# Attention and a gated FFN on one core: q and k laid out transposed by numpy, low parts on GpSimd, P divided on VectorE, V's product a step later

## The chip, the cores and the metric

The kernel runs on one core of one Trainium2 chip. The metric is device time in microseconds, the median of three runs. The engines are called as the profile calls them: PE (TensorE; PEld is its weight load), DVE (VectorE), ACT (ScalarE), POOL (GpSimd) and SP (SyncE, whose queue issues nearly all DMAs).

## What is computed

Eight-head attention over 4 sequences of 768 tokens with head size 64, with a window of 96 keys and 8 global keys and a linear bias by distance, and behind it an FFN whose gate is a ratio of polynomials:

```
scores = q @ k.T / 8 - slope[h] * dist          # where keep, else -1e9
a = exp(scores - max); a = a / (sum(a) + 1e-9)
x = (a @ v) as [3072, 512]
h = x @ w_in                                    # [512, 2048], float64 input
g = (a0 + a1*h + a2*h**2 + a3*h**3) / (1 + |b0|*|h| + |b1|*h**2 + 1e-6)
out = g @ w_out                                 # [2048, 512], float64 input
```

## The kernel before

The work is cut in two streams that are woven together. A **unit** u is one pair of heads (p, two heads x = 0, 1) for 128 query rows (block i of a sequence); 96 units, 8 to a chunk of 256 tokens. An **FFN tile** f is 256 of the 2048 hidden columns for one chunk; also 96. A loop over steps t issues each unit's stages and, with a lag that `turn(f)` gives (10 steps at first, growing to LAG = 13 between tiles 16 and 24), each tile's stages. A scheduler then sets each engine's order from the priorities (1000 for a step plus the numbers in PRI), so the built order is not the order of the code.

The first 24 units (PLAIN) run in plain float32. From unit 24 on, q and k are split in a high part that PE takes in its reduced-precision float32 format (fp32r) and a low part, so that a score is two matmuls (line 439). For these units the stages are:

- `st_load` (L137): q and k of two units come as they lie in memory, `nat`; `st_move` (L146) copies them within SBUF through a DMA into `mv`, whose type PE may transpose.
- `st_qkT` (L377): four PE transposes for two units, `tk` in PSUM (L384), through the identity `ident_r`.
- `st_qkE` (L396): for each unit and each of its heads ACT writes the high part into `kq` (L416, 64 partitions, q and k side by side) and DVE the low part into the other 64 partitions (L417), both with the factor 2^(p-1). Two DMAs then build `qT` with the halves exchanged (L421, L422).
- `st_score` (L427): four score matmuls (L439), then DVE adds the mask (bf16, scaled by the head's slope) and takes the row maximum (L453). Before this, POOL puts the 8 global keys in (L444).
- `st_soft` and `st_sums`: exponentials on ACT (L463), sum and reciprocal on DVE (L468, L470).
- `st_norm` (L472): POOL divides P, two instructions of 128x256 for a unit (L479).
- `st_turn` (L495): DVE turns P in 32x32 blocks (L504), a DMA writes it to DRAM (`put`), and `st_back` (L511) reads it back with the blocks exchanged (`pT`).
- `st_pv` (L525): V's product for four units at once (L541), issued at step u + 8; `st_x` splits x into `xh` and `xl` (L570, L571).

The FFN tile f goes through `st_ffn1` (24 matmuls, L272), `st_ew1` (three ACT instructions from `h`), `st_ew2` (L303, L304 on DVE; the sum `fa` on POOL, L305), `st_ew3` (1/Q as exp(-log) on ACT, L312, L313), `st_ew4` (L317 to L319 on DVE, `g` high on ACT, L327, `g` low on POOL, L328) and `st_ffn2` (12 matmuls, L348). The weights are decoded and split (`split_w`, L223, L224) in the first 180 us.

Of the kernel before, what the change touches and what calls it, by code (L numbers as in the profile page):

```python
# [19 lines left out]
G = 8  # L20
# [6 lines left out]
LAG = 13  # L27
# [51 lines left out]
def window_masks(nc, scr, mask0, masks, nl, ng):  # L79
# [24 lines left out]
    nc.vector.tensor_copy(out=masks[:, 2, :], in_=masks[:, 0, :])  # L104
# [3 lines left out]
def tile_kernel(ctx: ExitStack, tc: tile.TileContext, q, k, v, n_global, n_local,  # L108
# [28 lines left out]
    def st_load(u, other=nc.sync):  # L137
        c, t, p, b, i = unit(u)
        hs = slice(2 * p, 2 * p + 4)
        r = slice(i * P, (i + 1) * P)  # L140
        n = pl.ldp.tile([P, 2, 4, D], F32, tag="nat", name=f"nat{u}")
        nc.sync.dma_start(out=n[:, 0], in_=q[b, hs, r, :].rearrange("h s d -> s h d"))
        other.dma_start(out=n[:, 1], in_=k[b, hs, r, :].rearrange("h s d -> s h d"))
        nat[u // 2] = n

    def st_move(u):  # L146
        n = pl.late.tile([P, 2, 4, D], FR, tag="moved", name=f"mv{u}")
        nc.sync.dma_start(out=n.bitcast(F32), in_=nat[u // 2])
        nat[u // 2] = n
# [246 lines left out]
    def st_qkE(u):  # L396
# [30 lines left out]
    def st_score(u):  # L427
# [3 lines left out]
        for x in range(2):  # L431
# [5 lines left out]
            rhs = pl.kq[:, h, 0:2, :] if i else pl.kq[:, h, 0:1, :].broadcast_to([P, 2, P])  # L437
            for z, lhsT in enumerate((pl.kq[:, h, 2, :], qT[:, x, :])):
# [3 lines left out]
        elif 1 <= i < NT - 1:  # L442
            hs = slice(2 * p, 2 * p + 2)
            nc.gpsimd.tensor_copy(out=pl.kq[:, hs, i % 2, 0:G], in_=pl.kG[:, hs, :])  # L444

        def mask(x):
            m0, m = (mask0, masks) if u < PLAIN or x == 0 else (pl.half0, pl.halves)
            return m0 if i == 0 else m[:, 0:2, :] if i % 2 else m[:, 1:3, :]
        pr = pl.att.tile([P, 2, 2, P], F32, tag="prob", name=f"pr{u}")
        st = stats[:, u % 4]  # L450
        for x in range(2):
# [125 lines left out]
    def windowed(lates):  # L577
# [18 lines left out]
        nc.vector.tensor_copy(out=ident_r, in_=ident)  # L596
        one = pl.early.tile([1, P], F32, name="one")
# [9 lines left out]
        window_masks(nc, scr, mask0, masks, nl, ng)  # L607
# [4 lines left out]
        def halve_masks():  # L612
            for m, full_m in ((pl.halves, masks), (pl.half0, mask0)):
                nc.vector.tensor_scalar(out=m, in0=full_m, scalar1=0.5, scalar2=None, op0=ALU.mult)

        def turn(f):
            return f + EARLY_LAG + (LAG - EARLY_LAG) * min(max(f - 2 * FPC, 0), FPC) / FPC

        f = -1
        for t in range(NU + LAG + F2 + 1):  # L620
# [22 lines left out]
            if t % 2 == 0:  # L643
                on("load", st_load, t + 4)
# [8 lines left out]
            if t == PLAIN:  # L653
                scope.close()
                pl.late = lates.enter_context(tc.tile_pool(name="late", bufs=1))
                pl.kq = pl.late.tile([P, H, 3, P], FR, name="kq")
                pl.kG = pl.late.tile([P, H, G], FR, name="kG")
                pl.halves = pl.late.tile([P, 3, P], BF16, name="halves")
                pl.half0 = pl.late.tile([P, P], BF16, name="half0")
# [207 lines left out]
```

## Time and profile before

| | us |
|---|---|
| median of 3 runs | 732.49 (732.41 to 733.73) |
| the profiled execution | 732.77 |
| its span, first to last instruction | 730.9 |
| PE busy | 706.0 (97%) |
| DVE busy | 604.1 (83%) |
| ACT busy | 577.1 (79%) |
| POOL busy | 457.5 (63%) |

A row of a view of groups gives line, engine, operation, the tiles it writes and reads, shape, count, then busy time in us and the mean of one in ns, then the engine's idle time before it and what ended it. Matmuls overlap in their records, so how long PE takes for one is read from start to start in the timeline. The sum of busy times says which engine is near its limit; the windows say in which stretch.

### The profile page before, as it was taken

To read this page: it belongs to the slowest core of one execution; us is meant where nothing else is said; L and a number is where in the kernel's file an instruction comes from. 1 tells how busy PE (TensorE), PEld (TensorE's weight loads), DVE (VectorE), ACT (ScalarE), POOL (GpSimd) and SP (SyncE) were. 2 spreads that over 40 slices of the span, in tenths; PEclk is the share of its full clock that TensorE was granted. 3 is DMA by queue.
4 is the path that set the end of the run, shared out by engine and by line. 5 is a ranking of instruction groups with operands and counts; after the bars stand their busy time and mean duration, and the time that the engine had idled before them with its cause. 6 is when DMAs were issued, how large, how long until landed. Compare 5 with 4: busy or idle time off the path is not lost.

```text
span 730.9 us, 14868 instructions
## 1 busy us (share of the span) xinstructions
PE 706.0 (97%) x4762; PEld 608.0 (83%) x4762; DVE 604.1 (83%) x1508; ACT 577.1 (79%) x1304; POOL 457.5 (63%) x504
## 2 busy tenths in 40 slices
PE   5898999999999999999999999999999999999996
PEld 4575666788978889988988998998998998988894
DVE  5789966789889898888889889898889988875664
ACT  6798576977988788888887878887888878865764
POOL 3275986767567675665566657665667666754441
PEclk9999999999999999999999999999999999999998
DMA  9987210114564654645536455665346454421001
GB/s 265 294 278 215 89 23 22 52 23 105 157 166 133 200 154 130 182 141 154 142 111 181 140 136 166 173 183 137 98 121 197 138 160 129 118 88 30 30 1 34
DMA packets 139899, 96.76 MB, mean 132 GB/s; under 512 B 84260, under 2 KB 124196, under 8 KB 139812
## 3 DMA queue, kind: packets, MB, share of 16 engines
q1 hardware_dynamic: 138608, 95.20, 45.4%
q8 instruction: 40, 0.66, 0.4%
q10 hardware_dynamic: 1204, 0.52, 0.3%
q14 instruction: 47, 0.39, 0.2%
HBM read 53.22 MB, written 23.59 MB: 105 GB/s over the span
## 4 chain that ended last, share of the span: by engine, by line
PE 83%; DVE 6%; ACT 5%; DMA 2%; issue 2%; POOL 0%; SPq 0%; DVEq 0%; ACTq 0%; POOLq 0%
PE h L272 32%; PE acc L348 32%; PE o L541 5%; PE s L439 4%; PE acc L343 2%; PE h L264 2%; PE s L434 2%; DMA r<-in_moe_w_in_dram 1%; ACT pr L463 1%; PE tk L384 1%; PE tp L492 1%; DVE fu L303 1%; DVE fu L319 1%; DVE pr L453 1%; DMA nat<-in_q_dram 1%
## 5 line engine op out<-in xcount | busy, mean ns | idle before, releaser
L272 PE MATMUL h<-xh,win_l 128*128 128x256 f32 x704 | 197.1, 280 | 0.0
L479 POOL TENSOR_SCALAR pr<-pr,stats 128x256 f32<-128x256 f32 (+1 forms) x176 | 156.2, 898 | 59.5 <-DVE stats L470 37.0
L305 POOL TENSOR_TENSOR fa<-fa,fs 128x512 f32<-128x512 f32 x95 | 123.7, 1302 | 92.0 <-ACT fs L298 86.5
L348 PE MATMUL acc<-wout_l,g 128*128 128x512 f32 x352 | 139.3, 396 | 0.0
L328 POOL TENSOR_TENSOR g<-fu,g 128x512 fp32r<-128x512 f32 x87 | 113.9, 1309 | 33.9 <-ACT g L327 31.1
L272 PEld LDWEIGHTS h<-xh,win_l 128*128 128x128 f32 x704 | 133.2, 189 | 1.8 <-issue 0.5
L463 ACT ACTIVATE pr<-pr,stats 128x256 f32<-128x256 f32 (+1 forms) x192 | 93.1, 488 | 18.5 <-DVE stats L453 17.2
L296 ACT ACTIVATE fu<-h,coef 128x512 f32<-128x512 f32 (+1 forms) x97 | 74.9, 772 | 39.5 <-PE h L272 34.5
L317 DVE SCALAR_TENSOR_TENSOR fu<-fu,coef,q 128x512 f32<-128x512 f32 (+1 forms) x97 | 71.4, 736 | 32.5 <-ACT q L313 30.6
L312 ACT ACTIVATE fs<-fa,coef 128x512 f32<-128x512 f32 (+1 forms) x97 | 69.6, 717 | 22.5 <-POOL fa L305 21.1
L303 DVE TENSOR_TENSOR fu<-fu,h 128x512 f32<-128x512 f32 (+1 forms) x97 | 65.0, 671 | 21.0 <-ACT fs L298 20.7
L348 PEld LDWEIGHTS acc<-wout_l,g 128*128 128x128 f32 x352 | 66.2, 188 | 11.8
L304 DVE SCALAR_TENSOR_TENSOR fu<-fu,coef,h 128x512 f32<-128x512 f32 (+1 forms) x97 | 71.4, 736 | 1.9
L318 DVE SCALAR_TENSOR_TENSOR q<-fa,coef,q 128x512 f32<-128x512 f32 (+1 forms) x97 | 72.1, 743 | 0.0
L417 DVE SCALAR_TENSOR_TENSOR kq<-tk,kq 64x256 fp32r<-64x256 f32 x144 | 60.6, 422 | 10.9 <-ACT kq L416 6.7
L416 ACT ACTIVATE kq<-tk 64x256 fp32r<-64x256 f32 x144 | 54.2, 376 | 19.2 <-DVE kq L417 13.6
L297 ACT ACTIVATE fa<-h,coef 128x512 f32<-128x512 f32 (+1 forms) x97 | 65.6, 676 | 1.4 <-DMA out_dram<-o 1.3
L298 ACT ACTIVATE fs<-h,coef 128x512 f32<-128x512 f32 (+1 forms) x97 | 66.2, 682 | 0.3 <-DVE q L318 0.2
L319 DVE SCALAR_TENSOR_TENSOR fu<-q,fu 128x512 f32<-128x512 f32 (+1 forms) x97 | 65.2, 672 | 1.3
L327 ACT CAST g<-fu 128x512 fp32r<-128x512 f32 (+1 forms) x89 | 54.9, 616 | 13.3 <-DVE fu L319 12.2
L504 DVE STREAM_TRANSPOSE tb<-pr 128x256 f32<-128x256 f32 (+1 forms) x144 | 58.7, 414 | 5.7 <-POOL pr L479 2.0
L313 ACT ACTIVATE q<-fs 128x512 f32<-128x512 f32 (+1 forms) x97 | 57.3, 591 | 2.0 <-DVE stats L470 0.6
(257 smaller groups left out, 1943.8 us busy)
## 6 DMA issues: line engine op xcount, KB each, us to landing
put<-tb SPq DMA_DIRECT2D x30, 512.0 KB
pT<-put SPq DMA_DIRECT2D x120, 128.0 KB
mv<-nat SPq DMA_DIRECT2D x36, 256.0 KB
qT<-kq SPq DMA_DIRECT2D x144, 64.0 KB
r<-in_moe_w_in_dram SPq DMA_DIRECT2D x16, 512.0 KB
r<-in_moe_w_out_dram SPq DMA_DIRECT2D x16, 512.0 KB
nat<-in_q_dram SPq DMA_DIRECT2D x48, 128.0 KB
vt<-in_v_dram SPq DMA_DIRECT2D x48, 128.0 KB
```

The lines of the kernel that those rows point to most:

```text
L272: nc.tensor.matmul(out=hps[f][:, y, :], lhsT=w[:, fs], rhs=x[:, ct, :], start=(n == 0), stop=(n == 3 * NCT - 1))
L296: nc.scalar.activation(out=u, in_=h, func=AF.Identity, scale=a3, bias=a2)
L303: nc.vector.tensor_tensor(out=u, in0=u, in1=h, op=ALU.mult)
L304: nc.vector.scalar_tensor_tensor(out=u, in0=u, scalar=a1, in1=h, op0=ALU.add, op1=ALU.mult)
L305: side(f).tensor_tensor(out=a, in0=a, in1=s, op=ALU.add)
L317: nc.vector.scalar_tensor_tensor(out=u, in0=u, scalar=a0, in1=r, op0=ALU.add, op1=ALU.mult)
L318: nc.vector.scalar_tensor_tensor(out=r, in0=a, scalar=q1, in1=r, op0=ALU.add, op1=ALU.mult)
L319: nc.vector.scalar_tensor_tensor(out=u, in0=r, scalar=2.0, in1=u, op0=ALU.subtract, op1=ALU.mult, reverse0=True)
L328: side(f).tensor_tensor(out=g[:, 1, ys], in0=u, in1=g[:, 0, ys], op=ALU.subtract)
L348: nc.tensor.matmul(out=acc, lhsT=gs[f][:, z, y, ts], rhs=w, start=(ft == 0 and n == 0), stop=(ft == NFT - 1 and n == 2))
L463: nc.scalar.activation(out=d, in_=d, func=AF.Exp, scale=-1.0, bias=st[:, x:x + 1], accum_out=st[:, 2 + 2 * x:3 + 2 * x])
L479: nc.gpsimd.tensor_scalar(out=d, in0=d, scalar1=st[:, 6 + x:7 + x], scalar2=None, op0=ALU.mult)
```

## The change

From unit 24 on:

- numpy builds one more input, `qk`, in which q and k of four heads stand already transposed, [128 of two heads' dimensions, (k, q), two units, 128 rows]. One DMA of 2 KB a partition loads it for two units, two steps ahead instead of four. `st_move`, the four transposes and `tk` are gone.
- `st_split` takes the place of `st_qkE` and works on two units at once: two ACT casts of 64x512 from SBUF, and two subtractions of 64x512, now on POOL. The factor 2^(p-1) is dropped; in its place each head has its own copy of the mask, scaled on DVE once at step 24 (seven instructions). `qT` is built by two DMAs for two units, their priority 600 later, in place of four.
- The division of P (`st_norm`) is DVE's.
- `st_turn` turns a unit's two heads in one instruction of 512 columns.
- V's product is issued at t % 4 == 1, at step u + 9. LAG is 14, and `turn` lets the lag grow from tile 8 to tile 24 instead of from 16 to 24.

Before unit 24, and in the FFN, nothing is changed but the lag and where the mask lies.

```diff
-LAG = 13
+LAG = 14
...
+        if u >= PLAIN:
+            nat[u // 2] = pl.ldp.tile([P, 2, 2, P], F32, tag="nat", name=f"kq{u}")
+            nc.sync.dma_start(out=nat[u // 2], in_=qk[b, i, p // 2])
+            return
...
-    def st_move(u):
-        n = pl.late.tile([P, 2, 4, D], FR, tag="moved", name=f"mv{u}")
-        nc.sync.dma_start(out=n.bitcast(F32), in_=nat[u // 2])
-        nat[u // 2] = n
...
-        if u >= PLAIN:
-            tk = pl.ps_t.tile([P, 2, 2, P], FR, tag="t", name=f"tk{u}")
-            for y in range(2):
-                for z in range(2):
-                    n = nat[u // 2][:, 1 - z, 2 * y:2 * y + 2, :]
-                    nc.tensor.transpose(out=tk[:, y, z, :], in_=n.rearrange("p a d -> p (a d)"), identity=ident_r)
-                tqk[u + y] = tk[:, y]
-            return
...
+    def st_split(u):
+        c, t, p, b, i = unit(u)
+        kq, raw = pl.kq, nat[u // 2]
         for x in range(2):
             own, other = slice(x * D, (x + 1) * D), slice((1 - x) * D, (2 - x) * D)
-            at = kq[:, 2 * p + x, i % 2:3:2 - i % 2, :]
-            nc.scalar.activation(out=at[own], in_=raw[own], func=AF.Copy, scale=half)
-            nc.vector.scalar_tensor_tensor(out=at[other], in0=raw[own], scalar=half, in1=at[own], op0=ALU.mult,
-                                           op1=ALU.subtract)
-        hs = slice(2 * p, 2 * p + 2)
-        qT = pl.late.tile([P, 2, P], FR, tag="qT", name=f"qT{u}", bufs=4)
-        nc.sync.dma_start(out=qT[0:D].bitcast(F32), in_=kq[D:P, hs, 2, :].bitcast(F32))
-        nc.sync.dma_start(out=qT[D:P].bitcast(F32), in_=kq[0:D, hs, 2, :].bitcast(F32))
+            at = kq[:, x, p // 2, i % 2:3:2 - i % 2]
+            nc.scalar.copy(out=at[own], in_=raw[own])
+            nc.gpsimd.tensor_tensor(out=at[other], in0=raw[own], in1=at[own], op=ALU.subtract)
+        tc.cur_priority += 600
+        qT = pl.late.tile([P, 2, 2, P], FR, tag="qT", name=f"qT{u}", bufs=2)
+        nc.sync.dma_start(out=qT[0:D].bitcast(F32), in_=kq[D:P, :, p // 2, 2].bitcast(F32))
+        nc.sync.dma_start(out=qT[D:P].bitcast(F32), in_=kq[0:D, :, p // 2, 2].bitcast(F32))
...
-            rhs = pl.kq[:, h, 0:2, :] if i else pl.kq[:, h, 0:1, :].broadcast_to([P, 2, P])
-            for z, lhsT in enumerate((pl.kq[:, h, 2, :], qT[:, x, :])):
+            kx = pl.kq[:, x, p // 2, :, p % 2, :]
+            rhs = kx[:, 0:2, :] if i else kx[:, 0:1, :].broadcast_to([P, 2, P])
+            for z, lhsT in enumerate((kx[:, 2, :], qT[:, x, :])):
...
-            nc.gpsimd.tensor_scalar(
+            (nc.vector if u >= PLAIN else nc.gpsimd).tensor_scalar(
                 out=d, in0=d, scalar1=st[:, 6 + x:7 + x], scalar2=None, op0=ALU.mult)
...
-            for x in range(2):
-                at = 2 * y + x
-                nc.vector.transpose(out=turned[:, :, at:at + 4 * W - 3:4, :].rearrange("p b w i -> p w b i"),
-                                    in_=pr[:, x, 0:W, :].rearrange("p w (b j) -> p w b j", j=Q))
+            at = turned[:, :, 2 * W * y:2 * W * (y + 1), :].rearrange("p b n i -> p n b i")
+            if i:
+                nc.vector.transpose(out=at, in_=pr.rearrange("p x w (b j) -> p (x w) b j", j=Q))
...
+        def scaled_mask(h):
+            if 0 <= h < H and h != 2:
+                nc.vector.tensor_scalar(out=masks[:, h], in0=masks[:, 2], scalar1=2.0 ** (2 - h), scalar2=None,
+                                        op0=ALU.mult)
...
-            return f + EARLY_LAG + (LAG - EARLY_LAG) * min(max(f - 2 * FPC, 0), FPC) / FPC
+            return f + EARLY_LAG + (LAG - EARLY_LAG) * min(max(f - FPC, 0), 2 * FPC) / (2 * FPC)
...
-                on("load", st_load, t + 4)
+                if t + 4 < PLAIN:
+                    on("load", st_load, t + 4)
+                if t + 2 >= PLAIN:
+                    on("load", st_load, t + 2)
...
-            if t % 4 == 0 and t - 8 >= PLAIN:
-                pv(t - 8, 0)
+            if t % 4 == 1 and t - 9 >= PLAIN:
+                pv(t - 9, 0)
...
-                on("qkE", st_qkE, t)
-                on("qkE", st_qkE, t + 1)
+                on("qkE", st_split, t)
```

In the rows of the built order below a name's number tells one buffer from another; `s` are scores, `h` and `acc` the FFN's sums, `fa` and `g` the FFN's sum on POOL and its result.

PE, in the middle of the attention stretch, around the scores of a pair, before:

```order
L348 MATMUL acc_0_5353<-wout_l,g_5266 128x512
L439 MATMUL s_5372<-kq,qT_5230 128x256
L439 MATMUL s_5372<-kq 128x256
L439 MATMUL s_5372<-kq,qT_5230 128x256
L384 MATMUL tk_5398<-ident_r,mv_5217 128x128 x4
L348 MATMUL acc_0_5353<-w_0h,g_5266 128x512
```

and after:

```order
L430 MATMUL s_5239<-kq 128x256
L430 MATMUL s_5239<-kq,qT_5006 128x256
L430 MATMUL s_5239<-kq 128x256
L430 MATMUL s_5239<-kq,qT_5006 128x256
L430 MATMUL s_5318<-kq 128x256
L430 MATMUL s_5318<-kq,qT_5192 128x256
L430 MATMUL s_5318<-kq 128x256
L270 MATMUL h_5068<-xh_4409,w_0_1h 128x256
```

The four transposes of a pair are gone, and scores of several units follow one another.

DVE, there, for about one unit, before:

```order
L453 ISA pr_5499,stats<-s_5493,halves 128x256
L453 ISA stats 128x1
L317 SCALAR_TENSOR_TENSOR fu_5466<-fu_5466,coef,q_5524 128x512
L318 SCALAR_TENSOR_TENSOR q_5524<-fa_5467,coef,q_5524 128x512
L468 TENSOR_REDUCE stats<-stats 128x2
L319 SCALAR_TENSOR_TENSOR fu_5466<-q_5524,fu_5466 128x512
L470 RECIPROCAL stats<-stats 128x2
L303 TENSOR_TENSOR fu_5541<-fu_5541,h_5506 128x512
```

and after:

```order
L301 TENSOR_TENSOR fu_5212<-fu_5212,h_5170 128x512
L458 TENSOR_REDUCE stats<-stats 128x2
L302 SCALAR_TENSOR_TENSOR fu_5212<-fu_5212,coef,h_5170 128x512
L460 RECIPROCAL stats<-stats 128x2
L469 TENSOR_SCALAR pr_5324<-pr_5324,stats 128x256 x2
L458 TENSOR_REDUCE stats<-stats 128x2
L494 STREAM_TRANSPOSE tb_5525<-pr_5324 128x4x4x32
L460 RECIPROCAL stats<-stats 128x2
L469 TENSOR_SCALAR pr_5406<-pr_5406,stats 128x256 x2
L315 SCALAR_TENSOR_TENSOR fu_5212<-fu_5212,coef,q_5270 128x512
```

The two divisions now follow the reciprocal at once, and those of a pair's two units stand close together, ahead of the FFN's L315.

POOL, there, before:

```order
L305 TENSOR_TENSOR fa_5542<-fa_5542,fs_5543 128x512
L479 TENSOR_SCALAR pr_5499<-pr_5499,stats 128x256 x2
L328 TENSOR_TENSOR g_5550<-fu_5466,g_5550 128x512
L444 COPY kq<-kG 128x2x8 x2
L305 TENSOR_TENSOR fa_5645<-fa_5645,fs_5646 128x512
L479 TENSOR_SCALAR pr_5579<-pr_5579,stats 128x256 x2
L328 TENSOR_TENSOR g_5653<-fu_5541,g_5653 128x512
```

and after:

```order
L303 TENSOR_TENSOR fa_5127<-fa_5127,fs_5128 128x512
L326 TENSOR_TENSOR g_5135<-fu_5026,g_5135 128x512
L434 COPY kq<-kG 128x2x8 x2
L303 TENSOR_TENSOR fa_5213<-fa_5213,fs_5214 128x512
L407 TENSOR_TENSOR kq<-kq_5314,kq 64x512 x2
L326 TENSOR_TENSOR g_5221<-fu_5126,g_5221 128x512
```

In place of two divisions a unit there are two subtractions a pair, and the low part of g stands behind them.

## Rows read from the trace of the kernel before

**Rows 1.** The page: busy time and share, and the chain by engine.

```profile
PE 706.0 (97%) x4762; PEld 608.0 (83%) x4762; DVE 604.1 (83%) x1508; ACT 577.1 (79%) x1304; POOL 457.5 (63%) x504
...
PE 83%; DVE 6%; ACT 5%; DMA 2%; issue 2%; POOL 0%; SPq 0%; DVEq 0%; ACTq 0%; POOLq 0%
```

**Rows 2.** Windows (stretch: length, busy us by engine); then line 439: ns min/median/max, first, last.

```profile
core 0: us, PE busy (x) PEld busy (x) DVE busy (x) ACT busy (x) POOL busy (x), PEclk, DMA share, GB/s
180.00:648.00 468.00, 465.36 (x3366) 419.01 (x3364) 410.06 (x1067) 386.57 (x865) 305.30 (x338) 1.00 0.53 149
185.00:240.00 55.00, 53.34 (x382) 47.30 (x382) 50.01 (x143) 48.17 (x114) 37.55 (x46) 1.00 0.58 160
650.00:700.00 50.00, 50.00 (x336) 44.44 (x335) 31.60 (x48) 33.60 (x56) 22.18 (x18) 1.00 0.10 33
...
L439 PE MATMUL s<-kq x144: 274/281/389, 179.4 to 647.6; 128*128 128x256 f32 x144
```

**Rows 3.** Timeline (start, length in us, instruction; in brackets idle before, releaser): PE.

```profile
219.21 0.50 PE L348 MATMUL acc<-w_6h,g 128*128 128x512 f32 x1 [1.57 <-ACT g L327]
```

**Rows 4.** Timeline of PE, 303 to 310 us; then two groups by line.

```profile
303.80 0.40 PE L348 MATMUL acc<-w_14h,g 128*128 128x512 f32 x1
...
305.43 0.40 PE L348 MATMUL acc<-w_15h,g 128*128 128x512 f32 x1
...
305.66 0.28 PE L272 MATMUL h<-xh,w_1h 128*128 128x256 f32 x1
...
308.37 0.28 PE L272 MATMUL h<-xh,win_l 128*128 128x256 f32 x1
...
308.96 0.28 PE L439 MATMUL s<-kq 128*128 128x256 f32 x1
...
309.08 0.46 PE L384 MATMUL tk<-ident_r,mv 128*128 128x128 f32 x4
...
309.38 0.35 PE L272 MATMUL h<-xh,w_1h 128*128 128x256 f32 x1
...
309.56 0.28 PE L272 MATMUL h<-xl,w_1h 128*128 128x256 f32 x1
...
L541 PE MATMUL o<-pT,vt 128*64 128x128 f32 x704 | 51.5, 281 | 0.0
...
L384 PE MATMUL tk<-ident_r,mv 128*128 128x128 f32 x144 | 16.8, 236 | 0.0
```

**Rows 5.** Groups by line, DVE.

```profile
L318 DVE SCALAR_TENSOR_TENSOR q<-fa,coef,q 128x512 f32<-128x512 f32 (+1 forms) x97 | 72.1, 743 | 0.0
...
L303 DVE TENSOR_TENSOR fu<-fu,h 128x512 f32<-128x512 f32 (+1 forms) x97 | 65.0, 671 | 21.0 <-ACT fs L298 20.7
L417 DVE SCALAR_TENSOR_TENSOR kq<-tk,kq 64x256 fp32r<-64x256 f32 x144 | 60.6, 422 | 10.9 <-ACT kq L416 6.7
```

**Rows 6.** Groups by line, POOL.

```profile
L479 POOL TENSOR_SCALAR pr<-pr,stats 128x256 f32<-128x256 f32 (+1 forms) x176 | 156.2, 898 | 59.5 <-DVE stats L470 37.0 <-ACT q L313 9.9 <-ACT kq L416 6.3
L305 POOL TENSOR_TENSOR fa<-fa,fs 128x512 f32<-128x512 f32 x95 | 123.7, 1302 | 92.0 <-ACT fs L298 86.5 <-issue 3.2 <-POOL pr L479 1.0
```

**Rows 7.** Timeline: casts on DVE beside POOL; then line 223, ns min/median/max.

```profile
104.74 0.43 DVE L223 CAST w_0h<-w_0f 128x512 fp32r<-128x512 f32 x1 [2.29 <-POOL win_l L224]
...
109.10 1.19 POOL L479 TENSOR_SCALAR pr<-pr,stats 128x256 f32<-128x256 f32 x1
...
109.16 0.43 DVE L223 CAST w_2h<-w_2f 128x512 fp32r<-128x512 f32 x1 [0.50 <-POOL wout_l L224]
...
141.69 1.29 POOL L328 TENSOR_TENSOR g<-fu,g 128x512 fp32r<-128x512 f32 x1
...
141.82 1.44 DVE L223 CAST w_3h<-w_3f 128x512 fp32r<-128x512 f32 x1
...
L223 DVE CAST w_2h<-w_2f x3: 415/427/428, 109.2 to 120.0; 128x512 fp32r<-128x512 f32 x3
...
L223 DVE CAST w_3h<-w_3f x2: 1116/1276/1436, 141.8 to 149.8; 128x512 fp32r<-128x512 f32 x2
```

More of the change, by code (lines that the diff above doesn't have):

```diff
@@ L103, in window_masks, with tile_kernel @@
         nc.vector.tensor_tensor(out=mask0[:, 0:G], in0=mask0[:, 0:G], in1=gm, op=ALU.max)
-    nc.vector.tensor_copy(out=masks[:, 2, :], in_=masks[:, 0, :])
 @with_exitstack
-def tile_kernel(ctx: ExitStack, tc: tile.TileContext, q, k, v, n_global, n_local,
+def tile_kernel(ctx: ExitStack, tc: tile.TileContext, q, k, qk, v, n_global, n_local,
                 w_in, w_out, ca, cb, out):
@@ L363, in tile_kernel @@
     ident = const.tile([P, P], F32, name="ident")
-    ident_r = const.tile([P, P], FR, name="ident_r")
-    mask0 = const.tile([P, P], BF16, name="mask0")
-    masks = const.tile([P, 3, P], BF16, name="masks")
+    masks = const.tile([P, H, 3, P], BF16, name="masks")
     sp = {}
@@ L442, in st_score @@
         elif 1 <= i < NT - 1:
-            hs = slice(2 * p, 2 * p + 2)
-            nc.gpsimd.tensor_copy(out=pl.kq[:, hs, i % 2, 0:G], in_=pl.kG[:, hs, :])
+            nc.gpsimd.tensor_copy(out=pl.kq[:, :, p // 2, i % 2, p % 2, 0:G], in_=pl.kG[:, :, p, :])
         def mask(x):
-            m0, m = (mask0, masks) if u < PLAIN or x == 0 else (pl.half0, pl.halves)
-            return m0 if i == 0 else m[:, 0:2, :] if i % 2 else m[:, 1:3, :]
+            m = masks[:, 2 * p + x if u >= PLAIN else 2]
+            return m[:, 2, :] if i == 0 else m[:, 0:2, :] if i % 2 else m[:, 1::-1, :]
         pr = pl.att.tile([P, 2, 2, P], F32, tag="prob", name=f"pr{u}")
@@ L519, in turned_p @@
         pT = pTs[u // 2 * 2]
-        return pT[:, :, 4 * w + 2 * (u % 2) + x, :] if u >= PLAIN else pT[:, u % 2, x, w, :]
+        W = 2 if unit(u)[4] else 1
+        return pT[:, :, 2 * W * (u % 2) + W * x + w, :] if u >= PLAIN else pT[:, u % 2, x, w, :]
     def run_of(u):
@@ L595, in windowed @@
             nc.gpsimd.memset(pl.qz[(1 - x) * D:(2 - x) * D, :, x, :], 0.0)
-        nc.vector.tensor_copy(out=ident_r, in_=ident)
-        one = pl.early.tile([1, P], F32, name="one")
+        one = tmp("one")[0:1, 0, 0:P]
         n1 = pl.early.tile([1, 4], F32, name="n1")
@@ L606, in windowed @@
         scr = [scr[:, x, :] for x in range(4)]
-        window_masks(nc, scr, mask0, masks, nl, ng)
+        window_masks(nc, scr, masks[:, 2, 2, :], masks[:, 2], nl, ng)
         load_coef()
         base = tc.cur_priority
-        def halve_masks():
-            for m, full_m in ((pl.halves, masks), (pl.half0, mask0)):
-                nc.vector.tensor_scalar(out=m, in0=full_m, scalar1=0.5, scalar2=None, op0=ALU.mult)
+        def scaled_mask(h):
+            if 0 <= h < H and h != 2:
+                nc.vector.tensor_scalar(out=masks[:, h], in0=masks[:, 2], scalar1=2.0 ** (2 - h), scalar2=None,
+                                        op0=ALU.mult)
         def turn(f):
-            return f + EARLY_LAG + (LAG - EARLY_LAG) * min(max(f - 2 * FPC, 0), FPC) / FPC
+            return f + EARLY_LAG + (LAG - EARLY_LAG) * min(max(f - FPC, 0), 2 * FPC) / (2 * FPC)
         f = -1
@@ L655, in windowed @@
                 pl.late = lates.enter_context(tc.tile_pool(name="late", bufs=1))
[L656 to L659, printed above, removed]
-                tc.cur_priority = base + 1000 * t
-                halve_masks()
-                on("split", st_move, t)
+                pl.kq = pl.late.tile([P, 2, 2, 3, 2, P], FR, name="kq")
+                pl.kG = pl.late.tile([P, 2, NPAIR, G], FR, name="kG")
+            if t == PLAIN:
+                for h in range(H):
+                    on("load", scaled_mask, h)
             ffn("ffn1a", st_ffn1, f, 0)
-            if t < PLAIN or t % 2 == 0:
+            if t < PLAIN:
                 on("qkT", st_qkT, t)
-            if t >= PLAIN and t % 2 == 0:
-                on("split", st_move, t + 2)
             if t % 2 == 0 and t - 4 >= PLAIN:
@@ L849, with turned @@
     from concourse.bass_utils import run_bass_kernel_spmd as _run
-    nc = _bacc.Bacc("TRN2", target_bir_lowering=False, num_devices=1, dynamic_dma_scratch_size=2048)
+    nc = _bacc.Bacc("TRN2", target_bir_lowering=False, num_devices=1, dynamic_dma_scratch_size=512)
     arrays, args = {}, []
+    def turned(a):
+        a = _np.asarray(a)
+        B, H, S, D = a.shape
+        return a.reshape(B, H // 4, 2, 2, S // P, P, D).transpose(0, 4, 1, 3, 6, 2, 5).reshape(B, S // P, H // 4, 2 * D, 2, P)
+    inputs = dict(inputs, qk=_np.stack([turned(inputs["k"]), turned(inputs["q"])], axis=4))
     for name in _INS:
```

16 lines of the change are left out of this document (8 added, 8 removed).

## The prediction

> **What bounds the kernel now.** I read the busy shares first, then the windows, then PE's waits, then single instructions. PE is busy for 97% of the span at full clock, and 83% of the chain that ended last lies on it [rows 1]. From the first two-part score to the last (179.4 to 647.6 us [rows 2], "the attention stretch" below) PE is busy for 465.4 of 468 us, DVE for 410.1, ACT for 386.6, POOL for 305.3 [rows 2]. In the densest part, 185 to 240 us, DVE is busy for 50.0 of 55 us, and there PE loses 1.7 us [rows 2], nearly all of it in one wait for ACT's g, 1.57 us [rows 3]. After 650 us PE is still full while DVE falls to 63% [rows 2]. So the time is the sum of what PE issues, plus little; DVE is next in line, at 88%.
>
> What PE issues is counted from start to start, since busy times of pipelined matmuls overlap. Twenty-four first-layer matmuls start from 305.66 to 308.37: 0.118 us each [rows 4]. Eight second-layer ones start from 303.80 to 305.43: 0.233 each [rows 4]. An FFN tile (24 and 12 of them) is 5.63 us. A unit of attention has four score matmuls, 0.47 us, and eight of V's product at 51.5/704 = 0.073, 0.59 us [rows 4]: 1.06 us. The built order has 67 FFN tiles and 72 units in the attention stretch: 377 + 76 + the transposes' 13 (below) = 466 us, beside 468 measured. The account closes.
>
> **The change part by part.**
> *The transposes of q and k go from PE.* From the score at 308.96, over four transposes, to the second matmul of the next kind at 309.56 is 0.60 us [rows 4]; two matmuls alone take 0.236, so four transposes cost 0.364 us. There are 144, so 36 x 0.364 = 13.1 us. Bounds: to the next matmul's start alone, 0.42 - 0.12 = 0.30 for four, 10.8 us; their whole busy time, 16.8 us [rows 4]. I take 13.1, which closes the account above. All of it is on the path: PE has nothing to wait for in their place. Base: 732.8 us (the profiled execution, 730.9 of span and 1.9 around it; 0.3 above the median of the runs) - 13.1 = 719.7.
>
> *DVE loses the low parts and gains the division.* Five FFN instructions of 0.67 to 0.74 us (the shortest and the longest stand in [rows 5]; the five sum to 3.56) overlap by some 0.08 each where they follow one another: 3.25 us a tile. So a unit costs DVE (410.1 - 67 x 3.25)/72 = 2.67 us. Out go two low parts of 0.42 [rows 5], 0.84. One 512-column transpose in place of two 256-column ones saves a start-up; I put it at 0.09, about the overlap above. Left are 1.74 us and the two divisions. Their price is not in the trace, since POOL does them now at 0.90 each [rows 6]. The nearest row of the same engine is the cast from SBUF to SBUF, 0.43 us for 512 columns with POOL idle [rows 7]; at half a nanosecond a column 256 take 0.29, the low end, 0.58 a unit. (At a nanosecond a column, and then with no waiting as I take it, they would take 0.42, 0.84 a unit: between the ends.)
>
> That cast is also what shows the danger. At 141.82 it stood behind a two-input POOL instruction that had begun at 141.69 and takes 1.29: it ended at 143.26, so it ran only once POOL was through [rows 7]. The sixteen casts (ten rows of this view, from 415 to 1436 ns, the undisturbed and the worst of them in [rows 7]) have a mean of 0.66: 0.24 of waiting for each. After the change POOL's steady work is of that two-input kind: per FFN tile two of 1.30 [rows 6], per pair of units two new subtractions, which I price at the same 1.30 (64 partitions, 512 columns; the row has 128 partitions; a cost of half or of twice would change POOL by 47 or 94 us in 414, and it has room for either). That is (60 x 2.6 + 72 x 1.3)/414 = 60% of the time. The second division follows the first at once, when POOL has just let go, so I let only the first wait: a unit's divisions cost N = 0.58 + 0.24 = 0.82 us. Ends: 0.58 (no waiting) and 0.58 + 2 x 0.60 x 0.65 = 1.36 (both wait out half of a POOL instruction in 60% of cases).
>
> The Trainium skill has a rule here (SBUF — State Buffer, "Who interferes with whom"): a VectorE instruction in a 2-port mode, tensor_scalar among them, and GpSimd hold the shared ports exclusively for a whole instruction, and the later one is fully blocked. Behind POOL's two-input instruction the trace agrees (1.44 us instead of 0.43); behind its one-input division it does not, since a cast issued 0.06 us after it took 0.43 as ever [rows 7]. By the rule to the letter the divisions take the upper end, which is the second rival below.
>
> *Where DVE then stands.* The built order puts 60 FFN tiles beside the 72 units (20, not 12, follow the last score), because the FFN now lags from tile 8 on and by 14. PE needs 60 x 5.63 + 72 x 1.06 = 414 us there, DVE 60 x 3.25 + 72 x (1.74 + 0.82) = 379, 92%. But attention is bunched. The first 6 tiles carry 12 units: PE 46.5, DVE 40.4 + 12N = 50.2, and PE waits 3.7. The last 18 carry 26: PE 128.9, DVE 103.7 + 26N = 125.0, 97%; at 91% PE lost 1.7 before, so I charge 1.6. The two parts between (18 tiles with 16 and with 18 units) stay under 90% and cost nothing. The 20 tiles at the end are pure FFN, which PE does without a gap today [rows 2]. Sum: 719.7 + 3.7 + 1.6 = **725.0 us**.
>
> *The rest, at nothing.* ACT makes 72 casts of 64x512 in place of 144 of 64x256; it waits for PE, at 83%. POOL gives up 144 divisions (130 us) and takes 72 subtractions (94). On SP's queue 36 copies and half of the qT transfers go, and one load takes the place of two; none of it stands on PE's chain today. The seven scaled masks come once, on DVE. V's product comes a step later on PE and has its pT earlier. If this cover fails, it shows as PE waiting for scores or g (third rival).
>
> **The rivals.**
> 1. *Nothing waits.* N = 0.58: the first part still costs 0.9, and the 2.6 us that PE loses in the stretch today go: 718.0. For it: POOL is freer, and the PSUM bank that the transposes took is free for scores. Against: DVE in the first part is at 102% even so.
> 2. *DVE becomes the bound, and it is slower.* The place is the two dense parts, the price the divisions behind POOL's subtractions. The loss is (40.4 + 12N - 46.5) + (103.7 + 26N - 128.9) = 38N - 31.3; it eats the 13.1 from N = 1.17, 0.59 for a division. At 1.36 it is 20.4: 740.1. For it: the order sets the divisions right behind the exponentials, while POOL is in the subtractions that follow ACT's casts. Against: only three of the sixteen casts took over 1 us.
> 3. *The new chain is late.* ACT's cast, POOL's subtraction and two transfers now end before a score, and on POOL the sums and the low parts of g are queued behind the subtractions; whoever needs g is PE. If a third of the 36 pairs makes PE wait as it does at 219.21 (1.57 [rows 3]), that is 19 us: 738.5. Against: a pair is split two steps ahead of its scores, some 11 us, and its two subtractions are 2.6.
> 4. *Both divisions wait like the casts:* N = 1.06, 6.6 + 2.4 lost, plus 1.6 as above: 730.3, at the edge of what can be told from no change.
>
> That the change does not do what it says is excluded by the built order: from unit 24 on PE has no transpose.
>
> **How the numbers follow.** Forecast 0.52 (720 to 730.5), rival 1 0.10, rival 4 and near it 0.12, rival 2 0.20, rival 3 0.06. A measurement here can tell 0.2%, 1.5 us. Faster: 0.52 + 0.10 = 0.62; rival 4 I split into 0.10 for no difference and 0.02 for slower; slower 0.28. The range reaches from rival 1, 718, to just past rival 2, 741; outside lie some 0.03 below and 0.10 above.
>
> **What would show it.** Right: no transposes of tk past 185 us, 414 us or a few more from the first two-part score to the last, a tail of 112 us of pure FFN; divisions on DVE of 0.29 alone and over 1 us behind POOL, 0.41 on average; DVE at 92% in the stretch; PE's gaps at its start, released by DVE or by ACT's g. Wrong: divisions above 0.59 on average and DVE at 97% or more (rival 2), PE's gaps released by qT's DMA or POOL (rival 3), or no waits at all (rival 1). The account falls if the score matmuls, which now read strided columns, start more than 0.118 apart.

## The result, and the profile after

The changed kernel takes 740.15 us (median of 4 runs, 739.61 to 741.82) beside 732.88 us of the kernel before on the same chip (732.41 to 733.73): 1.0102 times as long, 95% interval 1.0082 to 1.0122. It is 7.3 us slower where 7.8 us less were forecast. Of its page, busy times and the chain by engine; under them the windows (columns as in [rows 2]):

```profile
PE 704.2 (95%) x4618; PEld 596.5 (81%) x4618; DVE 609.9 (83%) x1440; ACT 568.7 (77%) x1231; POOL 429.4 (58%) x432
...
PE 76%; DVE 13%; ACT 4%; DMA 3%; issue 2%; POOL 1%; SPq 0%; ACTq 0%; DVEq 0%; POOLq 0%
```

```profile
172.00:600.00 428.00, 416.72 (x2924) 367.17 (x2923) 385.09 (x945) 346.12 (x742) 256.20 (x246) 1.00 0.49 138
200.00:500.00 300.00, 299.65 (x2091) 265.38 (x2089) 266.83 (x651) 245.28 (x515) 180.07 (x171) 1.00 0.48 135
500.00:600.00 100.00, 91.60 (x659) 79.55 (x656) 91.15 (x220) 76.35 (x170) 55.20 (x57) 1.00 0.55 149
600.00:700.00 100.00, 100.00 (x654) 86.86 (x653) 67.37 (x112) 66.17 (x113) 42.19 (x33) 1.00 0.10 33
```

Beside [rows 1], PE's share falls from 97 to 95%, and DVE's part of the chain doubles to 13%. The attention stretch is 428 us instead of 468, with a longer tail behind it, as the order has it. Most idle time stands in one place: PE is 91.6% busy from 500 to 600 us. From 200 to 500 it is as full as before, and this window hides half of the loss, as the account below shows. PE's waits that are new or have grown (total us, times, longest):

```profile
PE h L270 <- DVE fu L302: 3.1, 3, 1.4
PE o L533 <- DVE stats L443: 2.8, 1, 2.8
PE h L270 <- DVE stats L458: 2.3, 2, 1.7
PE acc L346 <- ACT g L325: 2.2, 2, 1.4
PE o L533 <- DMA pT<-put: 0.8, 1, 0.8
```

The divisions as a group (ns min/median/max); then, from the timeline, the worst of them, POOL beside it and the wait that followed:

```profile
L469 DVE TENSOR_SCALAR pr<-pr,stats x144: 270/352/1453, 176.9 to 613.0; 128x256 f32<-128x256 f32 x120, 128x128 f32<-128x128 f32 x24
```

```profile
546.57 2.67 POOL L407 TENSOR_TENSOR kq<-kq,kq 64x512 fp32r<-64x512 f32 x2
...
548.42 2.33 DVE L469 TENSOR_SCALAR pr<-pr,stats 128x256 f32<-128x256 f32 x2
...
549.32 1.29 POOL L303 TENSOR_TENSOR fa<-fa,fs 128x512 f32<-128x512 f32 x1
...
554.67 1.09 PE L533 MATMUL o<-pT,vt 128*64 128x128 f32 x16 [2.85 <-DVE stats L443]
```

Two divisions that take 0.35 us each alone lasted 2.33 us together: one behind POOL's subtraction, the other behind its L303. One us after them PE begins to wait, 2.85 us until 554.67, for DVE's L443, the reading of scores, which came late. That the divisions made it late is not shown by these rows; p1_acc below tests it.

**An account of PE.** PE's busy share cannot show where time goes between matmuls, so I counted each matmul from its start to the next one's, from 150 us on: its usual slot (0.118 us for h and s, 0.233 for acc, at most 0.103 for o), and what goes beyond. Each time V's product (o) begins or ends between other matmuls, three slots are longer than usual. The timeline of the changed kernel shows one such piece, of two matmuls:

```profile
297.07 0.39 PE L346 MATMUL acc<-wout_l,g 128*128 128x512 f32 x1
297.30 0.40 PE L346 MATMUL acc<-w_12h,g 128*128 128x512 f32 x1
297.53 0.39 PE L346 MATMUL acc<-wout_l,g 128*128 128x512 f32 x1
297.86 0.43 PE L533 MATMUL o<-pT,vt 128*64 128x128 f32 x2
298.22 0.39 PE L270 MATMUL h<-xh,w_0h 128*128 128x256 f32 x1
298.44 0.28 PE L270 MATMUL h<-xl,w_0h 128*128 128x256 f32 x1
298.56 0.28 PE L270 MATMUL h<-xh,win_l 128*128 128x256 f32 x1
```

The acc matmuls start 0.23 apart, but from the last of them to o it is 0.33; the first h after o has 0.22 to the next, the second 0.12. In the medians of the whole trace: 0.326 instead of 0.233 ahead of a piece (0.209 instead of 0.118 for h), 0.202 instead of 0.103 for the last matmul in it, 0.335 instead of 0.233 for the first acc behind it: 0.29 us a piece. The kernel before has the same slots, but cuts V's product less often. The account (us; long waits are those over 0.4 us each; "pieces" counts o's runs in the trace from 150 us on; what is left of each total, 542 to 546 us, is the usual slots):

| kernel | transposes | pieces: number, us | long waits | shorter ones | total from 150 us |
|---|---|---|---|---|---|
| before | 12.9 | 30, 8.2 | 3.2 | 6.6 | 573.8 |
| after | 1.1 | 58, 16.9 | 12.6 | 5.5 | 580.4 |
| p1_acc | 1.5 | 58, 17.0 | 4.0 | 5.1 | 573.1 |
| a1_whole | 1.5 | 22, 6.4 | 7.3 | 5.1 | 562.6 |
| c1_cut | 1.3 | 58, 16.9 | 7.2 | 8.0 | 575.6 |
| p3_whole | 1.5 | 23, 6.7 | 28.7 | 10.1 | 589.2 |

So the transposes gave 11.8 us, and two things took more: V's product in 28 pieces more (+8.7) and long waits (+9.4, of which 9.2 lie between 533 and 594 us). The last four rows are experiments. A sign of the pieces does stand on the page: the same 704 matmuls of V's product are busy for 59.9 us (L533), for 51.5 before (L541).

### The profile page after: what moved, and what is told of

Read it like the earlier page. It is cut to its first block, busy times and chain, and to the rows that moved or that the text cites. A ratio compares the mean times of both kernels' runs of the same rounds, so it can differ in the third digit from the quotient of the medians.

```text
span 737.8 us, 13978 instructions
## 1 busy us (share of the span) xinstructions
PE 704.2 (95%) x4618; PEld 596.5 (81%) x4618; DVE 609.9 (83%) x1440; ACT 568.7 (77%) x1231; POOL 429.4 (58%) x432
## 4 chain that ended last, share of the span: by engine, by line
PE 76%; DVE 13%; ACT 4%; DMA 3%; issue 2%; POOL 1%; SPq 0%; ACTq 0%; DVEq 0%; POOLq 0%
PE h L270 29%; PE acc L346 29%; PE o L533 5%; PE s L430 3%; DVE pr L469 3%; PE acc L341 2%; PE h L262 2%; PE s L424 2%; DVE pr L443 2%; DVE tb L494 1%; DVE q L316 1%; DVE fu L317 1%; DVE fu L301 1%; PE tp L482 1%; ACT pr L453 1%
## 5 line engine op out<-in xcount | busy, mean ns | idle before, releaser
L303 POOL TENSOR_TENSOR fa<-fa,fs 128x512 f32<-128x512 f32 x95 | 123.5, 1300 | 158.8 <-ACT fs L296 147.3
L407 POOL TENSOR_TENSOR kq<-kq,kq 64x512 fp32r<-64x512 f32 x72 | 93.5, 1298 | 20.4 <-ACT kq L406 4.7
L315 DVE SCALAR_TENSOR_TENSOR fu<-fu,coef,q 128x512 f32<-128x512 f32 (+1 forms) x97 | 70.9, 731 | 41.0 <-ACT q L311 40.6
L469 DVE TENSOR_SCALAR pr<-pr,stats 128x256 f32<-128x256 f32 (+1 forms) x144 | 83.8, 626 | 0.8
L533 PE MATMUL o<-pT,vt 128*64 128x128 f32 x704 | 59.9, 284 | 3.7 <-DVE stats L443 2.8
L533 PEld LDWEIGHTS o<-pT,vt 128*64 128x64 f32 x704 | 40.8, 137 | 21.7 <-issue 9.3
```

The costliest lines, as they stand in the source:

```text
L303: side(f).tensor_tensor(out=a, in0=a, in1=s, op=ALU.add)
L407: nc.gpsimd.tensor_tensor(out=at[other], in0=raw[own], in1=at[own], op=ALU.subtract)
L469: (nc.vector if u >= PLAIN else nc.gpsimd).tensor_scalar(out=d, in0=d, scalar1=st[:, 6 + x:7 + x], scalar2=None, op0=ALU.mult)
L533: nc.tensor.matmul(out=o_ps[x * D:(x + 1) * D, y, :], lhsT=vt[:, 2 * (y % 2) + x, :], rhs=turned_p(u0 + y, x, w), start=(n == 0), stop=(n ...
```

## The experiments

In the expectations T1 and T2 are two accounts of the loss. In the first four runs T1 is the forecast's second rival (the divisions wait for the port that DVE shares with GpSimd, and DVE becomes the bound) and T2 puts the loss down to the rest of the change, the later lag above all. After them T1 became: two separate terms, the pieces of V's product and the divisions' waits. Its rivals: pieces cost nothing of their own, or the scheduler's order makes the waits whatever the divisions do. (The expectations count 55 runs of V's product for the changed kernel and 19 or 20 for the joined ones; the traces, from unit 24 on, have one less.)

**One part undone at a time.** The edits, each against the changed kernel:

```diff
 e1_nodiv, in st_norm:
-        if u < DIVIDED:
+        if u < DIVIDED or u >= PLAIN:
             return
 e6_acc, in st_norm from unit 24 (junk: a cell that nobody reads):
-            nc.vector.tensor_scalar(out=d, in0=d, scalar1=st[:, 6 + x:7 + x], scalar2=None, op0=ALU.mult)
+            nc.vector.tensor_scalar(out=d, in0=d, scalar1=st[:, 6 + x:7 + x], scalar2=None, op0=ALU.mult,
+                                    op1=ALU.add, accum_out=junk[:, x:x + 1])
 e4_oldlag:
-LAG = 14
+LAG = 13
   (with the old ramp in turn(), and pv(t - 8, 0) at t % 4 == 0)
 e3_divpool, in st_norm:
-            (nc.vector if u >= PLAIN else nc.gpsimd).tensor_scalar(
+            nc.gpsimd.tensor_scalar(
```

e1_nodiv. 

> The changed kernel with the division of P left out from unit 24 on (the output there is not divided by the sum). Theory 1, the divisions on DVE, held up behind POOL's two-input instructions, make DVE the bound where attention is bunched: without them DVE has 80 us less to do, PE's gaps between 500 and 600 us go, and the time is 719 to 723 us. Theory 2, the bunching by the new lag and the later product of V is itself what makes PE wait: the gaps stay, 733 us or more.

Measured: 736.89 us (1.0067, 1.0047 to 1.0086).

e6_acc. 

> The changed kernel with the division on DVE in the form that also writes out a sum (into a cell that nobody reads). Theory 1, as far as it says that the divisions wait for POOL: in this form DVE is expected not to need the ports it shares with POOL, so each takes 0.42 to 0.50 us, alone or beside POOL, the longest under 0.6, and by 38N - 31.3 with N of 0.85 to 1.0 the time is 721 to 727 us. If it is the plain length of the division and not the wait that counts: the mean stays near 0.6, and the time near 740. Theory 2: near 738 to 740, whatever the divisions take.

Measured: 730.65 us (0.9971, 0.9959 to 0.9982), above the range expected, and still better than leaving the division out, which no theory of DVE's load allows.

e4_oldlag. 

> The changed kernel with LAG, its growth and the step of V's product as they were before (13, from tile 16 to 24, u + 8). Theory 1: the divisions still take some 0.6 us each, but units stand further apart, so that DVE catches up more often: 727 to 735 us. Theory 2: the loss goes whole, 719 to 724 us.

Measured: 736.17 us (1.0056, 1.0035 to 1.0077), in neither range.

e3_divpool. 

> The changed kernel with the division back on POOL. Theory 1: DVE keeps up as in the run without divisions, but POOL has 130 us more, 127 of the 129 us that PE takes for the last 18 FFN tiles with 26 units, so part of the gain goes to PE waiting for g: 723 to 731 us. Theory 2: 735 us or more.

Measured: 781.51 us (1.068, 1.0651 to 1.0709). POOL then has the divisions and the subtractions. Its windows (columns as above):

```profile
500.00:600.00 100.00, 92.03 (x615) 79.43 (x614) 62.69 (x142) 70.68 (x141) 66.79 (x69) 0.97 0.32 92
200.00:500.00 300.00, 274.26 (x1872) 241.45 (x1870) 206.95 (x530) 226.29 (x482) 242.44 (x253) 0.96 0.48 136
```

POOL is busy for 242 of 300 us, PE for 274: with the subtractions on POOL the divisions had to leave it. That much of the change hangs together. But T1 in its first form fell with e1_nodiv: 3.3 us came back where 17 to 21 were expected. Each of these edits also made the scheduler write another order, and the account turned up the pieces: 54 to 59 in e1, e4 and e6.

**V's product in one run.** The edit, in st_pv: the later pair's first matmul goes first, so that o cannot start before its last pT, and the rest is queued directly behind it.

```diff
-        for y in range(n_u):
+        held = ExitStack()
+        for y in (2, 3, 0, 1) if n_u == 4 else range(n_u):
...
-                    nc.tensor.matmul(...)
+                    ins = nc.tensor.matmul(...)
+                    if y == 2 and n == 0 and x == 0:
+                        held.enter_context(tc.issue_after(ins.ins))
+                        tc.cur_priority -= 100000
+        held.close()
+        tc.cur_priority += 100000 if n_u == 4 else 0
```

a1_whole (changed kernel with this). 

> The changed kernel with one thing altered: V's product of four units (L533) starts with a matmul of its later pair, so that it cannot start before the last pT is there, and the rest is queued directly behind it; from unit 24 it stands in 19 unbroken runs on TensorE where the changed kernel's program has 55. The divisions stay on DVE in their shared-port form. T1 (each piece costs TensorE about 0.26 us of slots at its two ends, fitted over the six traces so far): 36 pieces fewer x 0.26 = 9.4 us, so about 731 (728 to 734), with 'entry and exit' slots of V's product at about 6 us instead of 16.9. T2 (the number of pieces costs nothing of its own, the excess is the divisions' and TensorE's waits): 737 to 742. T3 (holding V's product back until its last pT and letting it block TensorE for 1.6 to 3.3 us at a time makes scores and FFN late): over 742.

Measured: 720.26 us (0.9829, 0.9815 to 0.9842): 19.9 us below the changed kernel and 12.4 below the one before. That is twice what was expected of the pieces. Of the 17.8 us that the account shrinks by, 10.5 are their ends, 5.7 waits (the order is new as well), and 2.0 shorter slots inside V's product; what the transposes' column has more takes 0.4 back.

a2_acc_whole (with e6's division). 

> As a1_whole, and with the division on DVE in the form that also sums into an unread cell (as in e6_acc, which gave 730.65 with 58 pieces). T1 (pieces at 0.26 us, and the division's wait for GpSimd's port as a second, separate term): 730.65 - 39 x 0.26 = 720.5 (718 to 724). T2 (pieces cost nothing): 729 to 733. T3 (V's product held back makes others late): over 733.

Measured: 719.29 us (0.9814, 0.98 to 0.9827), the fastest version here that computes the whole result, and only 1 us below a1_whole.

a3_acc_oldlag_whole. 

> As a2_acc_whole, with LAG 13, the ramp of the kernel before and V's product issued at u+8 as before. T1: the same pieces and the same division, 720.5 (717 to 724); if the lag matters by itself it shows here against a2 (T2: with the old lag V's product waits for its pT more often, TensorE waits 'o <- DMA pT' grow, 725 to 732).

Measured: 722.25 us (0.9859, 0.9844 to 0.9874), in T1's range.

a4_before_whole (the same edit in the kernel before). 

> The kernel before, with V's product in one run each (18 runs instead of 25 from unit 24). T1 (0.26 us a piece): 7 x 0.26 = 1.8 us less, about 731 (729.5 to 732.5). T2 (pieces cost nothing): 732 to 734. This gives the price of a piece on a kernel with no division on DVE and no new lag.

Measured: 731.08 us (0.9973, 0.9961 to 0.9985), 1.6 less for 7 pieces.

a7_half (without the two lines on cur_priority). 

> The changed kernel with V's product held back until its last pT, but not put ahead of the FFN: 44 runs on TensorE, between the changed kernel (55, 740.15) and a1_whole (19, 720.26). T1 (a piece costs 0.26 us of slots, and an order in which attention and FFN alternate evenly saves waits besides): 728 to 738. T2 (it is the holding back alone that gained, pieces cost nothing): 719 to 723.

Measured: 737.39 us (1.0075, 1.0054 to 1.0095), in T1's range.

a8_cut300 (kernel before, `tc.cur_priority += 300` ahead of each unit's matmuls). 

> The kernel before (no division on DVE, old lag) with V's product cut on purpose: each unit's eight matmuls have a later due time than the unit's before, so FFN matmuls go between; 85 runs instead of 25 from unit 24, and units and FFN tiles follow each other nearly as before. T1 (0.26 us a piece): 60 x 0.26 = 15.6 us more, about 748 (744 to 752). T2 (the number of pieces costs nothing of its own): 732 to 736.

Measured: 760.60 us (1.0394, 1.0373 to 1.0415), 28.2 more, and above T1's range. The account gives 17.3 of them to the ends of 59 more pieces (0.29 each) and 7.0 to waits: the pieces cost what was said, and waits come on top.

a9_whole_oldlag. 

> e4_oldlag (LAG 13, old ramp, V's product issued at u+8; 736.17) with V's product in one run each: 19 instead of 53. T1 (34 pieces x 0.26 = 8.8): about 727, and less if waits go too (721 to 728). T2 (pieces cost nothing): 734 to 738. Beside a3 (722.25, the same with the division in its summing form) it gives the port's wait under the old lag: T1 0 to 3 us.

Measured: 739.54 us (1.0076, 1.0049 to 1.0103), a miss. Few pieces alone don't make a fast kernel: PE waited for pT four times, and for DVE.

```profile
PE o L534 <- DMA pT<-put: 9.1, 4, 3.2
```

a5_nodiv_whole (a1_whole without divisions). 

> a1_whole (720.26, divisions on DVE in their shared-port form, 0.689 us mean) with the division left out from unit 24 (so P stays undivided): the whole price of the division on DVE, its waits for GpSimd included, where V's product is not cut. T1 (with V's product in one run, DVE has room: the divisions cost 0 to 3 us): 717 to 720.5. T2 (the divisions and their waits bound the stretch as the forecast's terms had it: 3.7 us and more): 716 or less. The scheduler's order differs from a1_whole's, which by itself may add a few us of waits.

Measured: 730.00 us (0.996, 0.9943 to 0.9976): 10 us slower than a1_whole with less to do, and above both ranges. The order was another again, and V's product stood on PE twice before its pT had come:

```profile
PE o L534 <- DMA pT<-put: 8.1, 2, 4.2
```

So an edit that lets the scheduler order anew can bring some 10 us of its own, and the remaining runs hold the order fixed.

**The same order, one thing changed.** The order of the changed kernel's instructions, on all five engines, is written down as a table and imposed by ordering edges. The table alone, with nothing else changed, was not run. But the traces of p1_acc and p2_nodiv have the changed kernel's sequence on PE, POOL and SP instruction for instruction, and on DVE and ACT, the divisions aside, but for up to five copies of the output that stand on the other engine; c1_cut differs from a1_whole on PE alone.

```diff
+        traced = nc.cur_bb.bb.instructions
+        for text in ORDER.values():
+            row = _np.frombuffer(_zlib.decompress(_b64.b85decode(text)), dtype="<u2")
+            for x, y in zip(row[:-1], row[1:]):
+                tc.add_manual_dep(traced[int(y)], traced[int(x)].name, ...NoSync...)
```

p1_acc (the division in e6's form, summing into st[:, x:x + 1]). 

> The changed kernel with every engine's order of instructions in the windowed part imposed by a table, the changed kernel's own; the only difference is that the 144 divisions on DVE also sum into a cell that nobody reads later, the form that waited for no GpSimd instruction in e6_acc. V's product stays in 55 runs. T1 (the shared-port waits of the divisions are a term of their own, about the six long TensorE waits of 533 to 594 us, 9.2 us): 729 to 733. T2 (those waits come from the order, in which attention's units come in bunches, and stay): 737 to 740.

Measured: 733.08 us (1.0007, 0.9996 to 1.0017): 7.1 us less than the changed kernel. The divisions of p1_acc, and its window of 500 to 600 us:

```profile
L470 DVE TENSOR_SCALAR_CACHE_REDUCE pr<-pr,stats x144: 341/474/481, 178.6 to 605.5; 128x256 f32<-128x256 f32 x120, 128x128 f32<-128x128 f32 x24
```

```profile
500.00:600.00 100.00, 98.34 (x717) 85.71 (x714) 87.95 (x277) 81.42 (x180) 57.52 (x59) 1.00 0.54 153
```

None took over 0.481 us where the other form reached 1.453, and the long waits fall from 12.6 to 4.0.

p2_nodiv. 

> The same imposed order, with the divisions left out (P stays undivided from unit 24). T1: the same waits go, 728 to 732, at most 2 us below p1_acc. T2: 736 to 740. If it comes out well below p1_acc, the division's bare 0.34 us matters by itself, not only its waits.

Measured: 733.25 us (1.0021, 1.001 to 1.0032), the same as p1_acc. Both lie just above T1's ranges. So the divisions' own work costs nothing in this order; their wait costs 7 us.

p3_whole (on PE alone each V product moved to where its last matmul stood). 

> The same imposed order, divisions as in the changed kernel; on TensorE alone the matmuls of each unit group's V product are brought together where the last of them stood (one of the 18 groups stays in two runs, as the whole one could not be reached in that order): 20 runs instead of 55, nothing else moved. T1 (0.26 us a piece, waits unchanged): 740.2 - 35 x 0.26 = 731 (729 to 733). T2 (pieces cost nothing, a1_whole's gain came from its other order alone): 738 to 741.

Measured: 748.31 us (1.0209, 1.0194 to 1.0223), a miss. The ends of the pieces fell from 16.9 to 6.7 us as expected, but the long waits rose to 28.7. One of them was a chain; in the timeline of SP's queue, DVE and PE:

```profile
595.31 0.29 SPq L537 DMA_DIRECT2D vt<-in_v_dram  x1
...
597.07 0.55 SPq L498 DMA_DIRECT2D put<-tb  x1
...
600.59 0.71 DVE L494 STREAM_TRANSPOSE tb<-pr 128x512 f32<-128x512 f32 x1 [9.78 <-DMA put<-tb]
...
606.10 0.55 PE L270 MATMUL h<-xh,w_1h 128*128 128x256 f32 x1 [8.60 <-DVE fu L302]
```

SP's queue reloads the head of vt (L537) behind V's product. Pinned behind that reload stood the put (L498), DVE could not write tb again until it was through, and everything behind that transpose on DVE came late. The granted clock falls as well. In this trace it stands at half (0.50, the 1.2 GHz level) for 3.4, 3.4 and 6.8 us, each time at or just behind a long wait of PE; in the changed kernel's it does so nowhere in the attention stretch. The last of the three, at that chain (columns as above):

```profile
602.60:609.40 6.80, 3.30 (x15) 3.33 (x16) 6.80 (x19) 5.65 (x13) 1.29 (x1) 0.50 0.84 258
```

There first-layer matmuls start 0.213 us apart, not 0.118. By their slots the three cost 4.7 us, about the growth of the shorter waits from 5.5 to 10.1. So putting the pieces together paid only where the others' order went with it.

p4_acc_whole (both). 

> Both at once: the imposed order, the summing form of the division, V's product in 20 runs. T1 (two separate terms that add up: 9 of pieces, 8 to 10 of port waits): 720 to 724. T2 (only pieces count): 729 to 732. T3 (only port waits count): 729 to 733.

Measured: 734.77 us (1.0034, 1.0018 to 1.005), 13.5 below p3_whole, and a miss too: no range reached it. Its long waits are some 18 us instead of 28.7. That the divisions' waits cost more where the chain is late fits this, but is not shown by itself.

The last two impose a1_whole's own order instead.

c1_cut. 

> a1_whole (720.26, V's product in 19 runs, divisions in their shared-port form) with its own order imposed on every engine and one thing altered on TensorE: each V product is cut in three by drawing the next two FFN matmuls into it, one after the first third and one after the second: 55 runs as in the changed kernel, no matmul moved by more than 2 us. T1 (0.26 to 0.29 us a piece): 36 x 0.26 = 9.4 more, about 730 (728.5 to 731.5). T2 (the excess slots at the pieces' ends are paid for by something else, the count of pieces costs nothing): 720 to 723.

Measured: 733.52 us (1.0014, 1.0001 to 1.0026), 2 us above T1's range: 13.3 us more than a1_whole for 36 pieces, 0.37 each. Timeline of PE at one cut, and the window of 500 to 600 us in a1_whole and in c1_cut:

```profile
384.68 0.66 PE L534 MATMUL o<-pT,vt 128*64 128x128 f32 x8
385.26 0.49 PE L346 MATMUL acc<-wout_l,g 128*128 128x512 f32 x1
385.69 1.09 PE L534 MATMUL o<-pT,vt 128*64 128x128 f32 x16
386.71 0.50 PE L346 MATMUL acc<-w_4h,g 128*128 128x512 f32 x1
387.05 0.40 PE L346 MATMUL acc<-w_5h,g 128*128 128x512 f32 x1
387.28 0.40 PE L346 MATMUL acc<-wout_l,g 128*128 128x512 f32 x1
```

```profile
500.00:600.00 100.00, 100.00 (x707) 90.86 (x706) 93.89 (x212) 83.26 (x174) 63.94 (x63) 1.00 0.45 130
```

```profile
500.00:600.00 100.00, 100.00 (x700) 87.84 (x699) 91.55 (x207) 81.08 (x171) 58.85 (x57) 1.00 0.47 135
```

A lone acc inside V's product has 0.43 us to itself (385.26 to 385.69) instead of 0.23. Of the 13.0 us that PE's account grows by, 10.5 are ends of pieces and 2.9 the shorter waits, where the second of a lone matmul's two surcharges lands, and 1.5 us of a stretch at half the granted clock (183.6 to 187.0 us, behind a wait of 1.7) that a1_whole's trace does not have. PE is 100% busy in both windows: the price of a piece does not show in it, but in the number of matmuls, 707 and 700.

c2_nodiv. 

> a1_whole with its own order imposed on every engine and the divisions left out from unit 24. T1 (in this order DVE has room, the divisions and their waits of 0.69 us each are covered): 718 to 720.3. T2 (they cost here what they cost in the changed kernel's order, about 7 us): 711 to 714.

Measured: 718.30 us (0.9811, 0.9796 to 0.9826), 2.0 below a1_whole. In that order DVE, 93.9% busy, has room: the same divisions, waiting even longer (a mean of 0.67 us, 0.63 in the changed kernel), cost PE 2 us instead of 7.

## Why the prediction was wrong

**What bounds: right.** PE's issue plus its waits is the time, in every kernel here.

**The transposes: right.** 13.1 us were counted, 11.8 went.

**V's product "at nothing": the step that turned the sign.** The prediction priced its matmuls at 0.073 us each, wherever they stand, and asked only whether their pT would be there. It was: that wait is 0.8 us. What it left out is the number of runs. From unit 24 on V's product stands in 25 runs before and in 54 after, in the built orders as in the traces. The price lay in the trace of before too (0.326 us ahead of o), but 0.073 is busy time over all 704 matmuls, so the ends of the old runs were partly in it (within a run, from unit 24 on, a start follows the last by 0.056 us on average), and the account closed to 2 us. With 8.7 us for this, the forecast of 725.0 would have been 733.7, no change. What in the change makes the scheduler cut is only partly settled. Of orders that were built and not timed, the kernel before with the new lag and ramp alone has 35 runs, with V's product a step later alone 46, with both 34; the changed kernel with neither (e4) has 50. So each part cuts V's product by itself, and the numbers do not add up. What in the new path of q and k does it stays open.

**The divisions: the mechanism right, the size too small.** N was put at 0.82 us a unit by letting only the first of two divisions wait. The trace has a mean of 0.626 for one (0.344 for a full-width one undisturbed, not 0.29), so N = 1.25; of the full-width ones the first in a row has 0.595, those behind it 0.677. The reason given, that POOL "has just let go", failed: POOL's next two-input instruction caught the second division, as at 549.32 above. The Trainium skill (SBUF — State Buffer, "Who interferes with whom") says that the later of the two is fully blocked. Followed to the letter, both divisions wait, and here they did: 63 of the 120 full-width ones began beside a POOL instruction, or within 0.05 us ahead of its start, with a mean of 0.906; the other 57 have 0.344. The same section exempts the form of tensor_scalar that also writes out its accumulator, and the trace of p1_acc agrees (0.481 at most). That POOL's one-input division holds nobody up was read from one cast; another of the same trace, issued 0.05 us behind such a division at 99.50 us, took 0.70. The sum does not rest on it, since POOL's steady work is two-input after the change. The cost of the waits is 7.1 us by p1_acc, against 3.7 + 1.6 in the forecast.

**The formula for DVE's loss: wrong in both directions.** 38N - 31.3 gives 16.2 us at N = 1.25, and 7.1 were lost. The first dense part, charged with 3.7, lost 1.3 (3.4 us of long waits up to 260 us, of which p1_acc keeps 2.1); the second, charged with 1.6, lost the rest. The formula treats each part as a sum that PE must wait out; what PE waits for are single late results, so the order decides: 7 us in the changed kernel's order, 2 in a1_whole's.

**The rivals.** The second named 740.1, and the time is 740.15, but its mechanism, priced there at 20.4 us, is worth 7.1. Of its two signs one came, divisions of 0.63 on average; DVE is at 90% in the stretch (385.1 of 428 us), not at 97. The larger part of the rest was the pieces, and that the number hit is luck. The third is out: PE never waits for qT, and for g 2.2 us in all. The sum with measured terms: 732.8 - 11.8 + 8.7 + 7.1 = 736.8, beside 739.6 for the profiled execution. Of the 2.8 left, 1.4 are longer slots inside the cut products; the other 1.4 are not resolved.

## What to carry to other kernels

Price an operation on a full engine by how often it is entered and left, not only by its own length: count its runs in the built order, and its neighbours' start-to-start slots in the trace, since the busy share shows neither. When an edit lets a scheduler write a new order, that order alone can be worth over 10 us here (the same work took 730.0 us in a5_nodiv_whole and 718.3 in c2_nodiv); before crediting a cause, hold the order fixed and change one thing. And a moved instruction may have a form that doesn't contend: the summing form took 0.13 us more each, and 0.08 for reading the sum, and gave 7 us back.

## What the runs showed of the hardware

- A run of V's product (fp32, 64 columns of weights) between FFN matmuls (fp32r, 128 columns) costs PE 0.29 us at its ends, 0.09 to 0.10 in each of three slots, and 0.37 measured by c1_cut with all that follows (waits and the granted clock).
- On DVE a tensor_scalar of 128x256 fp32 takes 0.344 us undisturbed and up to 1.45 beside GpSimd's two-input instructions; with accum_out it takes 0.474, with 0.08 more for reading the sum, and took 0.481 at most in 144 cases (p1_acc).
- After some long waits of PE the granted clock stood at half for 3.4 to 6.8 us (p3_whole); matmuls of 256 columns then start 0.213 us apart instead of 0.118.
- 719.29 us (a2_acc_whole) is 1.9% below the kernel before: the change paid with V's product in one run in that order. It did not with one run each in a9_whole_oldlag and p3_whole, where PE waited.
